# Plain float32 for the first group's second product, and silu written over h in PSUM

## The chip, the cores and the metric

The kernel runs on one core of one Trainium2 chip. The metric is the device time of one execution in microseconds (us). Before the change three runs took 1640.9, 1642.14 and 1642.24 us, a median of 1642.14.

## What is computed

Pooled attention (keys and values averaged over 8 neighbours, 8 batches, 8 heads, 576 positions of 64), then two MLPs on the 4608 rows of 512, with a hidden width of 2048. The first MLP has the silu, the second h * clip(h + 3, 0, 6) / 6:

```
def _moe_ref(x, w_in, w_out):
    h = x @ w_in
    g = h * (1.0 / (1.0 + np.exp(-h)))
    return (g @ w_out).astype(np.float32)

def _moe2_ref(x, w_in, w_out):
    h = x @ w_in
    g = h * np.clip(h + 3.0, 0.0, 6.0) / 6.0
    return (g @ w_out).astype(np.float32)

x = attention(q, k, v) as 4608 x 512
return _moe2_ref(_moe_ref(x, w_in1, w_out1), w_in2, w_out2)
```

The weights arrive as float64, so as pairs of 32-bit words, and are made into float32 on the chip.

## The kernel before

The 4608 rows are 36 tiles of 128, in 9 groups of 4 tiles (512 rows). The hidden width is 16 blocks f of 128. The program has three stages: the attention of the first four tiles (to about 33 us), the first MLP group by group with the attention of the next group's tiles woven in (to about 920 us), and the second MLP by a Strassen-like scheme (to the end). The change touches the first MLP.

An iteration (g, f) of the first MLP issues, in this order and by hand, since the schedule is the order of the code:

- TensorE (PE): `h_mm`, 12 matmuls of 512 columns into one of two PSUM banks (`hps`, L479). Operands are float32r; each is split into a high and a low part (`xh`, `xl`, and `whl` for weights), and three of the four partial products are taken.
- ScalarE (ACT) and VectorE (DVE): `act_a` takes tanh(h/2) (L491) and (tanh + 1) * h (L492) into an SBUF tile `t`; `act_b` splits it into `gh` (ACT, L500) and `gl` = t - gh (DVE, L501).
- PE: `y_mm` of the iteration before (`pend`), 12 matmuls (L522), three partial products for each of four banks `y0` to `y3`. After the last f, `y_out` empties those banks (L532 on ACT, L534 on DVE), and the next group's first `y_mm` writes them again.

In the first group (g = 0) the first MLP's 32 weight tiles are also made, in the order of `pieces`: in-tile f, out-tile f - 1, and so on. A tile's 512 KB of words land in `wraw` (two words an element). `split_a` makes float32 of them: L108 on ACT, L111 and L114 on DVE, then either L121 on DVE or, with `mul`, L110 on ACT and L119 on GpSimd (POOL). The result, `wmag`, one of 4 buffers, goes to `split_b`: L131 on ACT copies the high part into `whl`, L132 on POOL subtracts the low part. `whl` takes the place of `wraw`. `share` says how many tiles an iteration converts: 1 to 3.

From the second group on the same iterations convert the second MLP's weights in small pieces (L156 to L178), at their own pace.

The attention of tile t in group 0 goes in threes of iterations: scores (L340) in the first, transposes of the probabilities (L404) in the second, the weighted sum (L444) and the split of x (L460, L461) in the third. The normalising (L388 to L393 on DVE) ends the first.

The tile `t` has two buffers, taken in turn. A buffer is free for the next writer when its last reader is done.

```
def act_a(layer, ps):                                        # before
    t = p2.tile([P, GT], F32, tag="t", name="t")             # two buffers
    nc.scalar.activation(t2, h, AF.Tanh, scale=0.5)          # ACT, reads PSUM
    nc.vector.scalar_tensor_tensor(out=t2, in0=t2, scalar=1.0, in1=h, ...)
def act_b(layer, g, f, t):
    nc.scalar.activation(gh, t, AF.Copy)
    nc.vector.tensor_tensor(out=gl, in0=t, in1=gh.bitcast(F32), op=ALU.subtract)
```

Of the kernel before, what the change touches and what calls it, by code (L numbers as in the profile page):

```python
# [25 lines left out]
def kernel(  # L26
# [57 lines left out]
    def dealt(ps):  # L84
        return ps.rearrange("p (n a) -> p a n", a=2)

    def in_two(ap):
        return ap.rearrange("p (a n) -> p a n", a=2)
# [12 lines left out]
    def split_a(layer, f, piece, mul=False):  # L101


        raw = w_raw.pop((layer, f, piece))
        hw = raw[:, :, 1]
        mag = att.tile([P, DM], F32, tag="wmag", name="wmag", bufs=4)
        bits = mag.bitcast(U32)
        nc.scalar.activation(mag, hw.bitcast(F32), AF.Copy, scale=2.0 ** -112)  # L108
        if mul:
            nc.scalar.activation(hw.bitcast(F32), hw.bitcast(F32), AF.Sign)  # L110
        nc.vector.tensor_scalar(  # L111
            out=bits, in0=bits, scalar1=3, scalar2=None, op0=ALU.logical_shift_left
        )
        nc.vector.scalar_tensor_tensor(  # L114
            out=bits, in0=raw[:, :, 0], scalar=29, in1=bits,
            op0=ALU.logical_shift_right, op1=ALU.bitwise_or,
        )
        if mul:
            nc.gpsimd.tensor_tensor(out=mag, in0=mag, in1=hw.bitcast(F32), op=ALU.mult)  # L119
        else:  # L120
            nc.vector.scalar_tensor_tensor(  # L121
                out=bits, in0=hw, scalar=0x80000000, in1=bits,
                op0=ALU.bitwise_and, op1=ALU.bitwise_or,
            )
        w_mag[layer, f, piece] = mag

    def split_b(layer, f, piece):

        mag = w_mag.pop((layer, f, piece))
        t = wts.tile([P, 2, DM], F32R, tag=f"{'io'[piece]}{f}", name="whl")  # L130
        nc.scalar.activation(t[:, 0, :], mag, AF.Copy)  # L131
        nc.gpsimd.tensor_tensor(out=t[:, 1, :], in0=mag, in1=t[:, 0, :].bitcast(F32), op=ALU.subtract)  # L132
        if piece == 0:
            t = t.rearrange("p a (c f) -> p a c f", f=P)
        w_sl[layer, f, piece] = (t[:, 0], t[:, 1])
# [337 lines left out]
    def h_mm(layer, g, f):  # L473
        ih, il = w_sl[layer, f, 0]
        xh, xl = xs[layer * NG + g]
        ps = ps_h.tile([P, GT], F32, tag="h", name="hps")
        for n, (w, x) in enumerate(((ih, xh), (il, xh), (ih, xl))):
            for c in range(NKC):
                nc.tensor.matmul(  # L479
                    ps,  # L480
                    w[:, c, :],
                    shuffled(x[:, c, :]),
                    start=(c == 0 and n == 0),
                    stop=(c == NKC - 1 and n == 2),
                )
        return ps

    def act_a(layer, ps):
        t = p2.tile([P, GT], F32, tag="t", name="t")
        t2, h = in_two(t), dealt(ps)  # L490
        nc.scalar.activation(t2, h, AF.Tanh, scale=0.5)  # L491
        nc.vector.scalar_tensor_tensor(  # L492
            out=t2, in0=t2, scalar=1.0, in1=h, op0=ALU.add, op1=ALU.mult
        )
        return t

    def act_b(layer, g, f, t):
        gh = p2.tile([P, GT], F32R, tag="gh", name="gh")
        gl = p2.tile([P, GT], F32R, tag="gl", name="gl")
        nc.scalar.activation(gh, t, AF.Copy)  # L500
        nc.vector.tensor_tensor(out=gl, in0=t, in1=gh.bitcast(F32), op=ALU.subtract)  # L501
        g_t[layer, g, f] = (gh, gl)


    FIRST = (0, 1)
    LAST = (NF - 1, NF - 2)

    def y_mm(layer, g, f):
        gh, gl = g_t.pop((layer, g, f))
        oh, ol = w_sl[layer, f, 1]  # L510
        if f == FIRST[layer]:
            y_ps[layer, g] = [
                ps_y.tile([P, 512], F32, tag=f"y{i}", name=f"y{i}") for i in range(4)
            ]
        for i, ps in enumerate(y_ps[layer, g]):
            sl = slice(i * P, (i + 1) * P)
            if layer == 0:
                prods = ((oh[:, sl], gh), (ol[:, sl], gh), (oh[:, sl], gl))
            else:
                prods = ((gh[:, sl], oh), (gh[:, sl], ol), (gl[:, sl], oh))  # L520
            for n, (a, b) in enumerate(prods):
                nc.tensor.matmul(  # L522
                    ps, a, shuffled(b), start=(f == FIRST[layer] and n == 0),
                    stop=(f == LAST[layer] and n == 2),
                )
# [126 lines left out]
    with tc.manual_schedule():  # L652
# [105 lines left out]
        for layer in range(1):  # L758
            for g in range(NG):
                todo = stages(g)  # L760
                if g == NG - 1:
                    early.close()
                    open_late()
                for f in range(NF):
                    n = (layer * NG + g) * NF + f
                    now = dict(todo[f])
                    load_ahead(2)
                    if n >= NF:
                        while ahead2 and len(half_raw) < 3:
                            load_half(*ahead2.pop(0))  # L770
                    while later:
                        later.pop(0)()
                    ps = h_mm(layer, g, f)
                    if 1 in now:
                        t1 = now[1]
                        scores(t1)
                        if t1 + 1 < NTILE:
                            load_q(t1 + 1)
                    if 3 in now:
                        pv = weighted(now[3])  # L780
                    tt = act_a(layer, ps)
                    quota = share[n] if n < NF else 2
                    due = len(done)
                    conv_a(1, 0)
                    for job in jobs_b:
                        job()
                    jobs_b = []
                    act_b(layer, g, f, tt)
                    if NF <= n < (NG - 1) * NF and SPLITTING[f] and jobs:
                        key, jobs_b = jobs.pop(0)  # L790
                        if key:
                            half_a(*key)
                    if g == NG - 1:
                        if f == 0:
                            load_x1(0)
                        elif f % 2 == 0 and f < 12:
                            make_x(0, f // 2 - 1)
                    conv_b(due)
                    if 1 in now:
                        new_pr(t1)  # L800
                        below_max(t1, 0)
                        below_max(t1, 1)
                        exps(t1, 0)
                        exps(t1, 1)
                    if 3 in now:
                        split_x(now[3], pv)
                    if n < 3:
                        for j in ((0, 1), (2,), (3,))[n]:
                            pool_k(1, j)
                    if 1 <= n < 5:  # L810
                        pool_v(1, n - 1)
                    if pend is not None:
                        y_mm(*pend)
                        if pend[2] == NF - 1:
                            y_out(*pend[:2])
                    pend = (layer, g, f)
                    conv_a(quota - 1, 1)
                    if 1 in now:
                        norm(t1)
                    if 4 in now:  # L820
                        vector_T(now[4])
                    if 2 in now:
                        probs_T(now[2])
                    if n >= 5 and f % 2 == 1:
                        for b, j in kv_wait:
                            pool_k(b, j)
                            pool_v(b, j)
                        kv_wait = []
                        if kv_jobs and f % 4 == 1 and TPG * (g + 1) + f // 4 + 4 >= first_tile[kv_jobs[0][0]]:
                            b, j = kv_jobs.pop(0)  # L830
                            load_k(b, j)
                            load_v(b, j)
                            kv_wait.append((b, j))
                    s = n - (NG - 1) * NF - 1
                    if 0 <= s < NF:
                        if s < 4:
                            load_factor(0, PASSING[s])
                        else:
                            load_factor((s - 4) // 3, STAYING[(s - 4) % 3])
                        load_split(s)  # L840
# [134 lines left out]
```

## Time and profile before

| | before |
|---|---|
| median of three runs | 1642.14 us |
| the profiled execution | 1641.74 us |
| its span, first to last instruction | 1639.9 us |
| PE busy | 1585.7 us (97%) |
| DVE, ACT, POOL busy | 1029.6, 632.9, 383.5 us |
| mean granted clock of PE | 0.989 of full speed |

A busy PE is not a PE at its peak, and the share over the whole span hides that the stages differ: in the first 180 us PE has gaps and a granted clock under 1, after that hardly any. Rows name a line, an engine, an operation and out<-in; the bracket after a row is the idle time in front of it and what ended it.

### The profile page before, as it was taken

The numbers are of one execution on the slowest core, as the hardware profiler recorded it, in microseconds if no ns is written. First come the engines' busy times: TensorE is split into PE (matmuls) and PEld (weight loads), VectorE is DVE, ScalarE is ACT, GpSimd is POOL, SyncE is SP. The second block draws the span as 40 slices with busy tenths as digits, with TensorE's granted clock in tenths as the row PEclk, the third lists the DMA queues.
The fourth block names the chain that finished last, engine by engine and source line by source line (L and its number), as shares of the span: only waits on it lengthen the run. The fifth ranks groups of instructions, "written<-read, shape, count | busy, mean of one in ns | idle before, by whom it ended". The sixth has DMA issues, their size and how long they took to land.

```text
span 1639.9 us, 24118 instructions
## 1 busy us (share of the span) xinstructions
PE 1585.7 (97%) x9312; PEld 1409.8 (86%) x9312; DVE 1029.6 (63%) x1608; ACT 632.9 (39%) x1094; POOL 383.5 (23%) x377
## 2 busy tenths in 40 slices
PE   7786999999999999999999999999999999999999
PEld 6565888888888888888888899999999999999998
DVE  6999677676766677675632455555555555656464
ACT  5345433333333333333322333333443343433333
POOL 4755222221322132311111011212121203020200
PEclk9899999999999999999999999999999999999999
DMA  9251334443444444433255634343435343535341
GB/s 316 78 197 37 109 99 162 133 153 124 147 143 138 136 135 140 157 126 123 70 179 201 228 114 155 104 159 111 154 107 160 107 154 103 157 100 167 102 130 52
DMA packets 101330, 224.27 MB, mean 137 GB/s; under 512 B 10464, under 2 KB 35936, under 8 KB 101216
## 3 DMA queue, kind: packets, MB, share of 16 engines
q1 hardware_dynamic: 101216, 222.73, 41.7%
q8 instruction: 73, 1.20, 0.3%
q14 instruction: 41, 0.34, 0.1%
HBM read 169.74 MB, written 52.95 MB: 136 GB/s over the span
## 4 chain that ended last, share of the span: by engine, by line
PE 77%; DVE 13%; DMA 3%; ACT 3%; issue 2%; SPq 0%; ACTq 0%; DVEq 0%
PE y L522 40%; PE hps L479 19%; PE p L597 16%; PE aps L340 1%; PE aps L444 1%; DVE u L864 1%; ACT gh L620 1%; DVE wmag L111 1%; DVE gl L621 1%; DVE gl L501 1%; DVE wmag L114 1%; DVE t L613 1%; DVE kbd L271 1%; DVE wmag L121 1%; ACT t L612 1%
## 5 line engine op out<-in xcount | busy, mean ns | idle before, releaser
L479 PE MATMUL hps<-x,whl 128*128 128x512 f32 x1728 | 398.7, 380 | 4.2 <-POOL whl L132 2.1
L597 PEld LDWEIGHTS p<-xst,wst 128*128 128x128 f32 x3024 | 359.6, 192 | 14.9 <-DVE u L864 7.8
L479 PEld LDWEIGHTS hps<-x,whl 128*128 128x128 f32 x1728 | 327.2, 190 | 51.7 <-POOL whl L132 2.5
L597 PE MATMUL p<-xst,wst 128*128 128x256 f32 x3024 | 363.2, 275 | 4.5 <-DVE u L864 4.5
L522 PE MATMUL y<-gh,whl 128*128 128x512 f32 x1152 | 358.6, 393 | 1.5 <-POOL whl L132 1.1
L522 PE MATMUL y<-whl,gh 128*128 128x512 f32 x1152 | 343.1, 379 | 0.6 <-ACT gh L620 0.6
L522 PEld LDWEIGHTS y<-gh,whl 128*128 128x128 f32 x1152 | 218.0, 194 | 37.9 <-issue 5.4
L522 PE MATMUL y<-gl,whl 128*128 128x512 f32 x576 | 224.3, 389 | 14.0 <-DVE gl L501 13.9
L585 POOL TENSOR_TENSOR xst<-xr,xst 128x512 fp32r<-128x512 f32 x63 | 83.4, 1324 | 619.1 <-ACT xst L584 619.1
L522 PEld LDWEIGHTS y<-whl,gh 128*128 128x128 f32 x1152 | 207.3, 190 | 24.2 <-ACT gh L620 0.8
L522 PE MATMUL y<-whl,gl 128*128 128x512 f32 x576 | 218.4, 379 | 0.1
L621 DVE TENSOR_TENSOR gl<-t,gh 128x512 fp32r<-128x512 f32 x144 | 115.1, 799 | 131.4 <-ACT gh L620 131.4
L492 DVE SCALAR_TENSOR_TENSOR t<-t,hps 128x512 f32<-128x512 f32 x144 | 97.7, 678 | 153.7 <-ACT t L491 152.9
L491 ACT ACTIVATE t<-hps 128x512 f32<-128x512 f32 x144 | 85.7, 595 | 275.3 <-PE hps L479 275.0
L501 DVE TENSOR_TENSOR gl<-t,gh 128x512 fp32r<-128x512 f32 x144 | 128.4, 892 | 90.5 <-ACT gh L500 90.5
L174 POOL TENSOR_TENSOR hs<-hmag,hs 128x256 fp32r<-128x256 f32 x88 | 65.1, 744 | 470.8 <-ACT hs L173 398.5
L620 ACT ACTIVATE gh<-t 128x512 fp32r<-128x512 f32 x144 | 120.3, 835 | 127.1 <-DVE t L613 127.1
L500 ACT ACTIVATE gh<-t 128x512 fp32r<-128x512 f32 x144 | 90.7, 630 | 181.8 <-DVE t L492 181.1
L613 DVE SCALAR_TENSOR_TENSOR t<-t,u 128x512 f32<-128x512 f32 x108 | 90.9, 842 | 104.8 <-ACT t L612 104.8
L864 DVE TENSOR_TENSOR u<-u,p 128x512 f32<-128x512 f32 x180 | 120.0, 683 | 44.7 <-PE p L597 40.5
L612 ACT ACTIVATE t<-u,three 128x512 f32<-128x512 f32 x108 | 77.8, 720 | 172.2 <-DVE u L864 172.2
L522 PEld LDWEIGHTS y<-gl,whl 128*128 128x128 f32 x576 | 111.9, 194 | 34.3 <-DVE gl L501 17.8
(86 smaller groups left out, 1358.6 us busy)
## 6 DMA issues: line engine op xcount, KB each, us to landing
wst<-ws SPq DMA_DIRECT2D x156, 512.0 KB
ws<-hs SPq DMA_DIRECT2D x56, 256.0 KB
bl<-bT SPq DMA_DIRECT2D x28, 384.0 KB
x<-o SPq DMA_DIRECT2D x36, 256.0 KB
xr<-x SPq DMA_DIRECT2D x36, 256.0 KB
out_dram<-o SPq DMA_DIRECT2D x36, 256.0 KB
wraw<-in_moe_w_in_dram SPq DMA_DIRECT2D x16, 512.0 KB
wraw<-in_moe_w_out_dram SPq DMA_DIRECT2D x16, 512.0 KB
```

What stands on the lines that cost most here:

```text
L479: nc.tensor.matmul(ps, w[:, c, :], shuffled(x[:, c, :]), start=(c == 0 and n == 0), stop=(c == NKC - 1 and n == 2),)
L491: nc.scalar.activation(t2, h, AF.Tanh, scale=0.5)
L492: nc.vector.scalar_tensor_tensor(out=t2, in0=t2, scalar=1.0, in1=h, op0=ALU.add, op1=ALU.mult)
L500: nc.scalar.activation(gh, t, AF.Copy)
L501: nc.vector.tensor_tensor(out=gl, in0=t, in1=gh.bitcast(F32), op=ALU.subtract)
L522: nc.tensor.matmul(ps, a, shuffled(b), start=(f == FIRST[layer] and n == 0), stop=(f == LAST[layer] and n == 2),)
L597: nc.tensor.matmul(ps[:, j * HW:(j + 1) * HW], w[:, j, a, c, :], shuffled(x[:, b, c, :]), start=(j == 0 and n == 0 and c == 0), stop=(j == ...
L612: nc.scalar.activation(t, h, AF.Relu, bias=three)
L613: nc.vector.scalar_tensor_tensor(out=t, in0=t, scalar=6.0, in1=h, op0=ALU.min, op1=ALU.mult)
L620: nc.scalar.activation(oh, t3, AF.Copy)
L621: nc.vector.tensor_tensor(out=ol, in0=t3, in1=oh.bitcast(F32), op=ALU.subtract)
L864: nc.vector.tensor_tensor(out=out, in0=a, in1=b, op=ALU.add)
```

## The change

In the first group `y_mm` becomes `y_whole`: four matmuls instead of twelve, with both operands in plain float32, not split. `act_b` is not run there. The out-tiles of the first MLP are converted by `split_a` as before, but the last step writes the float32 values over the high words in `wraw` (every second word), and `y_whole` reads them there. `split_b` of these 16 tiles moves to the second group: `split_whole(f)`, at the start of iteration (1, f), copies the tile into a buffer of `t` (L140) and then splits it (L150 on ACT, L151 on POOL). From the second group on `act_a` writes (tanh + 1) * h over h in PSUM (L518), and `act_b` reads PSUM (L526, L527).

```diff
+        dst = raw[:, :, 1] if piece else None
...
         if mul:
-            nc.gpsimd.tensor_tensor(out=mag, in0=mag, in1=hw.bitcast(F32), op=ALU.mult)
+            nc.gpsimd.tensor_tensor(
+                out=mag if dst is None else dst.bitcast(F32), in0=mag, in1=hw.bitcast(F32),
+                op=ALU.mult,
+            )
         else:
             nc.vector.scalar_tensor_tensor(
-                out=bits, in0=hw, scalar=0x80000000, in1=bits,
+                out=bits if dst is None else dst, in0=hw, scalar=0x80000000, in1=bits,
...
+        if piece:
+            w_whole[f] = dst.bitcast(F32)
+        else:
+            w_mag[layer, f, piece] = mag
+    def split_whole(f):
+        mag = p2.tile([P, DM], F32, tag="t", name="wcopy")
+        nc.scalar.activation(mag, w_whole.pop(f), AF.Copy)
+        w_mag[0, f, 1] = mag
+        split_b(0, f, 1)
...
+        if (layer, f, piece) not in w_mag:
+            return
...
+        if g == 0:
+            nc.scalar.activation(in_two(t), dealt(ps), AF.Tanh, scale=0.5)
+            nc.vector.scalar_tensor_tensor(
+                out=in_two(t), in0=in_two(t), scalar=1.0, in1=dealt(ps), op0=ALU.add, op1=ALU.mult
+            )
+            return t
+        nc.scalar.activation(t, ps, AF.Tanh, scale=0.5)
         nc.vector.scalar_tensor_tensor(
+            out=ps, in0=t, scalar=1.0, in1=ps, op0=ALU.add, op1=ALU.mult
+        )
+        return ps
...
+        nc.scalar.activation(in_two(gh), dealt(ps), AF.Copy)
+        nc.vector.tensor_tensor(
+            out=in_two(gl), in0=dealt(ps), in1=in_two(gh).bitcast(F32), op=ALU.subtract
+        )
+    def y_whole(f):
+        t, w = g_t.pop((0, 0, f)), w_whole[f]
+        if f == 0:
+            y_ps[0, 0] = [ps_y.tile([P, 512], F32, tag=f"y{i}", name=f"y{i}") for i in range(4)]
+        for i, ps in enumerate(y_ps[0, 0]):
+            nc.tensor.matmul(
+                ps, w[:, i * P:(i + 1) * P], shuffled(t), start=(f == 0), stop=(f == NF - 1)
+            )
...
+                    if g == 1:
+                        split_whole(f)
                     ps = h_mm(layer, g, f)
...
-                    act_b(layer, g, f, tt)
+                    if g:
+                        act_b(layer, g, f, tt)
+                    else:
+                        g_t[0, 0, f] = tt
```

DVE in the first group, from the silu of f = 4 to that of f = 5. Before, where L492 is the silu, L111 to L121 convert weights and L501 is `gl`:

```order
L492 SCALAR_TENSOR_TENSOR t<-t,hps 128x512
L111 TENSOR_SCALAR wmag<-wmag 128x512
L114 SCALAR_TENSOR_TENSOR wmag<-wraw,wmag 128x512
L121 SCALAR_TENSOR_TENSOR wmag<-wraw,wmag 128x512
L501 TENSOR_TENSOR gl<-t,gh 128x512
L111 TENSOR_SCALAR wmag<-wmag 128x512
L114 SCALAR_TENSOR_TENSOR wmag<-wraw,wmag 128x512
L111 TENSOR_SCALAR wmag<-wmag 128x512
L114 SCALAR_TENSOR_TENSOR wmag<-wraw,wmag 128x512
L121 SCALAR_TENSOR_TENSOR wmag<-wraw,wmag 128x512
L492 SCALAR_TENSOR_TENSOR t<-t,hps 128x512
```

After, the same stretch, with the silu at L513 and the conversion at L113 to L126:

```order
L513 SCALAR_TENSOR_TENSOR t<-t,hps 128x512
L113 TENSOR_SCALAR wmag<-wmag 128x512
L116 SCALAR_TENSOR_TENSOR wmag<-wraw,wmag 128x512
L126 SCALAR_TENSOR_TENSOR wraw<-wraw,wmag 128x512
L113 TENSOR_SCALAR wmag<-wmag 128x512
L116 SCALAR_TENSOR_TENSOR wmag<-wraw,wmag 128x512
L113 TENSOR_SCALAR wmag<-wmag 128x512
L116 SCALAR_TENSOR_TENSOR wmag<-wraw,wmag 128x512
L126 SCALAR_TENSOR_TENSOR wraw<-wraw,wmag 128x512
L513 SCALAR_TENSOR_TENSOR t<-t,hps 128x512
```

`gl` is gone; the last step of the out-tiles writes `wraw`.

POOL at the end of the first group and the start of the second. Before (L132 is the low part of a weight tile, L119 the sign by multiplication, L281 to L283 the pooling of v, L174 the second MLP's weights):

```order
L132 TENSOR_TENSOR whl<-wmag,whl 128x512 x3
L119 TENSOR_TENSOR wmag<-wmag,wraw 128x512
L132 TENSOR_TENSOR whl<-wmag,whl 128x512 x2
L281 TENSOR_TENSOR vraw<-vraw 72x2x256
L282 TENSOR_TENSOR vraw<-vraw 72x2x128
L283 TENSOR_TENSOR vp_82<-vraw 72x128
L174 TENSOR_TENSOR hs<-hmag,hs 128x256
```

After (L151 is the low part now, L193 the second MLP's weights):

```order
L151 TENSOR_TENSOR whl<-wmag,whl 128x512 x2
L121 TENSOR_TENSOR wraw<-wmag,wraw 128x512
L300 TENSOR_TENSOR vraw<-vraw 72x2x256
L301 TENSOR_TENSOR vraw<-vraw 72x2x128
L302 TENSOR_TENSOR vp_82<-vraw 72x128
L151 TENSOR_TENSOR whl<-wcopy,whl 128x512 x4
L193 TENSOR_TENSOR hs<-hmag,hs 128x256
```

The subtractions of the out-tiles (`whl<-wcopy`) stand behind the first group, one an iteration.

ACT across the same border. Before (L491 tanh, L500 `gh`, L364 the exponentials of the next tile, L532 emptying `y0` and `y2`):

```order
L491 ACTIVATE t<-hps 128x512
L500 ACTIVATE gh<-t 128x512
L491 ACTIVATE t<-hps 128x512
L500 ACTIVATE gh<-t 128x512
L364 ACTIVATE pr_84<-pr_84 128x288 x2
L532 ACTIVATE o<-y_614 128x512
L532 ACTIVATE o<-y_616 128x512
L491 ACTIVATE t<-hps 128x512
```

After (L512 and L517 tanh, L526 `gh`, L140 and L150 the copies of `split_whole`):

```order
L512 ACTIVATE t<-hps 128x512
L140 ACTIVATE wcopy<-wraw 128x512
L150 ACTIVATE whl<-wcopy 128x512
L517 ACTIVATE t<-hps 128x512
L526 ACTIVATE gh<-hps 128x512
L383 ACTIVATE pr_84<-pr_84 128x288 x2
L572 ACTIVATE o<-y_597 128x512
L572 ACTIVATE o<-y_599 128x512
L140 ACTIVATE wcopy<-wraw 128x512
```

In the first iteration of the second group the tanh (L517) writes the buffer that the last `y_whole` of the first group reads, and the emptying of the y banks stands behind it.

## Rows read from the trace of the kernel before

**Rows 1.** Windows of three rounds: length, busy (count) PE, PEld, DVE, ACT, POOL, clock, DMA.
```profile
83.35:111.37 28.02, 22.70 (x120) 18.23 (x120) 27.00 (x32) 14.48 (x25) 16.44 (x11) 0.88 0.72 269
...
139.67:168.00 28.33, 21.09 (x104) 17.41 (x104) 27.26 (x34) 14.42 (x25) 14.81 (x11) 0.91 0.11 31
sum 84.65, PE 65.41 PEld 53.63 DVE 81.49 ACT 43.07 POOL 47.49; mean PE 21.80 PEld 17.88 DVE 27.16 ACT 14.36 POOL 15.83
```

**Rows 2.** Groups on PE, 83.35 to 168.0 us: busy, mean ns, idle before, releaser.
```profile
L522 PE MATMUL y<-gl,whl 128*128 128x512 f32 x36 | 16.8, 467 | 6.6 <-DVE gl L501 6.6
```

**Rows 3.** Groups on DVE, 83.35 to 168.0 us.
```profile
L114 DVE SCALAR_TENSOR_TENSOR wmag<-wraw,wmag 128x512 uint32<-128x512 uint32 x18 | 19.5, 1085 | 0.6
L121 DVE SCALAR_TENSOR_TENSOR wmag<-wraw,wmag 128x512 uint32<-128x512 uint32 x12 | 14.8, 1235 | 0.4
L501 DVE TENSOR_TENSOR gl<-t,gh 128x512 fp32r<-128x512 f32 x9 | 14.7, 1628 | 0.0
L111 DVE TENSOR_SCALAR wmag<-wmag 128x512 uint32<-128x512 uint32 x18 | 13.9, 773 | 0.0
L492 DVE SCALAR_TENSOR_TENSOR t<-t,hps 128x512 f32<-128x512 f32 x9 | 6.1, 682 | 0.1
```

**Rows 4.** Groups on POOL, 83.35 to 168.0 us.
```profile
L132 POOL TENSOR_TENSOR whl<-wmag,whl 128x512 fp32r<-128x512 f32 x18 | 30.3, 1704 | 28.2 <-ACT whl L131 28.2
L119 POOL TENSOR_TENSOR wmag<-wmag,wraw 128x512 f32<-128x512 f32 x6 | 7.8, 1294 | 6.2 <-ACT t L491 3.7 <-DVE wmag L114 2.6
```

**Rows 5.** Timeline of POOL and of DVE, 32 and 114 us: start, length.
```profile
32.10 1.27 POOL L132 TENSOR_TENSOR whl<-wmag,whl 128x512 fp32r<-128x512 f32 x1 [12.79 <-ACT whl L131]
...
113.31 1.93 POOL L132 TENSOR_TENSOR whl<-wmag,whl 128x512 fp32r<-128x512 f32 x1 [6.63 <-ACT whl L131]
114.05 1.74 DVE L501 TENSOR_TENSOR gl<-t,gh 128x512 fp32r<-128x512 f32 x1
115.72 0.42 DVE L111 TENSOR_SCALAR wmag<-wmag 128x512 uint32<-128x512 uint32 x1
116.17 0.69 DVE L114 SCALAR_TENSOR_TENSOR wmag<-wraw,wmag 128x512 uint32<-128x512 uint32 x1
```

**Rows 6.** Group `gl` on DVE, 33 to 83.35 us.
```profile
L501 DVE TENSOR_TENSOR gl<-t,gh 128x512 fp32r<-128x512 f32 x4 | 7.0, 1745 | 0.0
```

**Rows 7.** Timeline of PE: plain float32 (ident, kbd), then float32r (hps).
```profile
11.11 2.85 PE L328 MATMUL aps<-ident 128*128 128x128 f32 x24
13.79 4.09 PE L340 MATMUL aps<-kbd,stage 128*128 128x144 f32 x32
187.61 2.75 PE L479 MATMUL hps<-x,whl 128*128 128x512 f32 x12
```

**Rows 8.** Timeline of PE: the attention's part of a round.
```profile
83.58 1.04 PE L404 MATMUL aps<-ident,pr 128*72 128x128 f32 x8 [1.88 <-DVE pr L393]
88.07 1.05 PE L444 MATMUL aps<-pT,vp 72*64 72x64 f32 x28 [0.86 <-ACT pT L405]
97.97 1.44 PE L340 MATMUL aps<-kbd,qT 128*128 128x144 f32 x8
```

**Rows 9.** Timeline where the second group starts.
```profile
184.30 0.60 ACT L491 ACTIVATE t<-hps 128x512 f32<-128x512 f32 x1 [3.26 <-PE hps L479]
184.93 0.69 PE L522 MATMUL y<-gh,whl 128*128 128x512 f32 x2
186.32 0.69 DVE L501 TENSOR_TENSOR gl<-t,gh 128x512 fp32r<-128x512 f32 x1 [0.70 <-ACT gh L500]
189.11 1.06 ACT L532 ACTIVATE o<-y 128x512 f32<-128x512 f32 x2
190.20 0.59 PE L522 MATMUL y<-gh,whl 128*128 128x512 f32 x2
```

**Rows 10.** Window of the second group.
```profile
182.00:280.00 98.00, 97.07 (x506) 83.46 (x505) 68.23 (x124) 34.99 (x70) 23.55 (x29) 1.00 0.41 133
```

**Rows 11.** Group on PE, 182 to 911 us: matmuls on `gl`.
```profile
L522 PE MATMUL y<-gl,whl 128*128 128x512 f32 x508 | 193.1, 380 | 0.1
```

More of the change, by code (lines that the diff above doesn't have):

```diff
@@ L118, in split_a @@
         if mul:
-            nc.gpsimd.tensor_tensor(out=mag, in0=mag, in1=hw.bitcast(F32), op=ALU.mult)
+            nc.gpsimd.tensor_tensor(
+                out=mag if dst is None else dst.bitcast(F32), in0=mag, in1=hw.bitcast(F32),
+                op=ALU.mult,
+            )
         else:
             nc.vector.scalar_tensor_tensor(
-                out=bits, in0=hw, scalar=0x80000000, in1=bits,
+                out=bits if dst is None else dst, in0=hw, scalar=0x80000000, in1=bits,
                 op0=ALU.bitwise_and, op1=ALU.bitwise_or,
             )
-        w_mag[layer, f, piece] = mag
+        if piece:
+            w_whole[f] = dst.bitcast(F32)
+        else:
+            w_mag[layer, f, piece] = mag
+    w_whole = {}
+    def split_whole(f):
[3 more added lines that the diff above has]
+        split_b(0, f, 1)
     def split_b(layer, f, piece):
+        if (layer, f, piece) not in w_mag:
+            return
         mag = w_mag.pop((layer, f, piece))
@@ L486, in h_mm, with act_a, act_b @@
         return ps
-    def act_a(layer, ps):
+    def act_a(g, ps):
         t = p2.tile([P, GT], F32, tag="t", name="t")
-        t2, h = in_two(t), dealt(ps)
-        nc.scalar.activation(t2, h, AF.Tanh, scale=0.5)
+        if g == 0:
[5 more added lines that the diff above has]
+        nc.scalar.activation(t, ps, AF.Tanh, scale=0.5)
         nc.vector.scalar_tensor_tensor(
-            out=t2, in0=t2, scalar=1.0, in1=h, op0=ALU.add, op1=ALU.mult
+            out=ps, in0=t, scalar=1.0, in1=ps, op0=ALU.add, op1=ALU.mult
         )
-        return t
-    def act_b(layer, g, f, t):
+        return ps
+    def act_b(layer, g, f, ps):
         gh = p2.tile([P, GT], F32R, tag="gh", name="gh")
         gl = p2.tile([P, GT], F32R, tag="gl", name="gl")
-        nc.scalar.activation(gh, t, AF.Copy)
-        nc.vector.tensor_tensor(out=gl, in0=t, in1=gh.bitcast(F32), op=ALU.subtract)
+        nc.scalar.activation(in_two(gh), dealt(ps), AF.Copy)
+        nc.vector.tensor_tensor(
+            out=in_two(gl), in0=dealt(ps), in1=in_two(gh).bitcast(F32), op=ALU.subtract
+        )
         g_t[layer, g, f] = (gh, gl)
@@ L506 @@
     LAST = (NF - 1, NF - 2)
+    def y_whole(f):
[6 more added lines that the diff above has]
+            )
     def y_mm(layer, g, f):
+        if (layer, g) == (0, 0):
+            return y_whole(f)
         gh, gl = g_t.pop((layer, g, f))
@@ L780 @@
                         pv = weighted(now[3])
-                    tt = act_a(layer, ps)
+                    tt = act_a(g, ps)
                     quota = share[n] if n < NF else 2
```

## The prediction

> **What bounds the kernel now.** I read the windows first, since the page's shares mix stages. In the first MLP's first group one round of three iterations repeats: from one silu behind the normalising to the next such silu takes 28.0 to 28.3 us, and of the 84.65 us of three rounds DVE is busy 81.5 us, while PE's granted clock is 0.88 to 0.91 [rows 1]. So DVE sets the pace there. [...] Then the later groups: PE is busy 97.07 of 98 us in the second group, at a clock of 1.00, and from 182 to 911 us it waits 0.1 us in all for `gl` [rows 10, 11]. There PE sets the pace and the others have room.
>
> Why DVE is slow is read from durations. A `gl` takes 0.69 us where POOL is idle [rows 9] but 1.63 us in the rounds [rows 3]. The timeline shows how: one that started at 114.05 ended at 115.79, 0.55 us behind the end of POOL's subtraction at 115.24, and right after it the same engine's L111 and L114 take 0.42 and 0.69 us [rows 5], where their means are 0.77 and 1.09 [rows 3]. DVE waits out POOL's instruction. The silu, which has one operand in PSUM, stays at 0.68 [rows 3].
>
> [...]
>
> **The rounds.** Free durations: 0.69 for `gl`, L114 and (same form) L121, 0.42 for L111. Waiting for POOL in three rounds: `gl` 9 x (1.628 - 0.69) = 8.5, L114 18 x (1.085 - 0.69) = 7.1, L121 12 x (1.235 - 0.69) = 6.5, L111 18 x (0.773 - 0.42) = 6.4 us, together 28.5 [rows 3]. POOL's work there, with L132 at its free 1.27 us [rows 5]: 18 x 1.27 = 22.9, L119 7.8, and 47.5 - 30.3 - 7.8 = 9.4 for the pooling of v: 40.1 us [rows 1, 4]. That is 0.71 us of DVE waiting for each us of POOL work. The change takes out nine `gl` (6.2 us of own time) and nine of the 18 subtractions (11.4 us of POOL, so 8.1 us of waiting). DVE's 84.65 us become 70.4.
>
> Can PE follow? Plain float32: 24 rows of 128 columns in 2.85 us, 32 of 144 in 4.09 [rows 7]. In the program these are 12 and 16 matmuls, so each counts as two rows. With the last row's tail off (about 0.28), 4.09 gives 123 ns a row, 0.85 ns a column, 436 ns for 512 columns; the other row gives 112 ns, 447. A `y_whole` is eight rows, 3.5 us (3.6 by the other). Float32r is 12 in 2.75 [rows 7], 2.6 us from start to start, for `h_mm` and for the old `y_mm` alike. So a y costs PE 0.9 us more. A round on PE: 3 x 2.6 + 3 x 3.5 + attention (about 0.8, 1.05 and 1.2, and a wait of 0.86 for ACT) [rows 8] = 22.2 us, three 66.6. DVE at 70.4 stays the slower, but by 5%, so that each hitch of one meets the other; I add 1 us: 71.4, a gain of 13.3. Bounds: 6.2 if the other DVE instructions now wait for all that POOL still does (only `gl`'s own time goes), 18 if PE is the floor.
>
> **Before and after the rounds.** From the first silu to 83.35 us stand four iterations with four `gl` of 1.745 us [rows 6]; their own time is 2.8 us, and five out-tiles' subtractions leave POOL, 5 x 1.27 x 0.71 = 4.5. I take 6.8 (bounds 2.8 and 9.5). Behind the rounds the conversion is over and PE sets the pace: y(13), y(14) and y(15) cost 0.9 us more each, a loss of 2.7. ACT loses `gh` and a copy per iteration in this group; it was busy 43.1 of 84.65 us [rows 1], so that counts nothing. Writing every second word costs DVE and POOL nothing by my reading, since their input there already has that step; if it did, it would be part of the waiting, whose bounds stand.
>
> **The border to the second group.** Here the change adds a wait. The tanh of (1, 0) writes the `t` buffer of (0, 15), which the last `y_whole` reads; that y follows `h_mm` (1, 0) on PE. Before, tanh started at 184.30, y(0, 15) at 184.93 [rows 9]; now tanh starts when that y ends, 184.93 + 3.5 + 0.15 = 188.6 on the old time scale, 4.3 us later. Queued behind it are, on DVE, silu, `gl`, the maxima of the next tile, two emptyings of y banks; on ACT, `gh`, two exponentials, two emptyings. The first of ACT's ended at 189.11 + 0.53 = 189.64 [rows 9] and now ends at 193.95. `y_mm` (1, 0) writes that bank; PE wants it at 190.20 + 0.9 = 191.1. A stall of 2.9 us (bounds 0 and 3.8).
>
> **The second group.** 16 subtractions of 1.27 us and 32 copies of about 0.6 come in. ACT goes from 35 to 55 of 98 us, POOL from 24 to 44. At the rate above DVE waits 20.3 x 0.71 = 14.4 us more, 68.2 becomes 82.6 of 98 [rows 10], less what `gl` waited. The moved step issues no DMA; on POOL it goes ahead of the second MLP's subtractions (L193), whose stores then leave 1.3 us later, with nobody waiting for them in this stage. An iteration's weights are wanted only behind the next `h_mm`. I price a few late `gl` at 0.6 us (bounds 0 and 8). Silu in PSUM: no instruction more, and the bank is held until `gl` is done, but the next `h_mm` into it follows the y that needs that `gl` anyway: 0 (bounds -0.5 and 1). The second MLP is untouched: 0.
>
> **The sum**, against the profiled execution's 1641.7 us (span 1639.9 and 1.8 around it; 0.4 under the median): -13.3 - 6.8 + 2.7 + 2.9 + 0.6 = -13.9, so 1627.8, and 1628 on the median's scale.
>
> **Rivals.** First, the waiting nearly vanishes and PE is the floor: -18 - 9.5 + 2.7 + 2.9 + 0.6 gives 1620.8. For it: POOL would have long gaps; against: L132 and L119 still fall among the conversions. Second, waiting is only passed on: -6.2 - 2.8 + 6.2 gives 1639. For it: in rows 3 every two-operand instruction waits, whichever is nearest; against: POOL's work itself shrinks by a fourth. Third, the second group isn't covered: half a us lost in each of 16 iterations instead of 0.6 in all gives 1635; for it, DVE at 84%, and that ACT's copy needs a `t` buffer which POOL must have read; against, the 0.1 us of rows 11. Fourth, on the slower side: `y_whole` is dearer and PE becomes the bound of the first group. With y the cost of one, three rounds take 9y + 35 us, the sum is 9y + 35 - 84.65 - 6.8 + 3(y - 2.6) + 3.5 = 12y - 61 us; it turns positive at y = 5.1 us, 635 ns a row instead of 436, and passes the limit of what can be told at 5.4. [...] For it: the clock of 0.88 and the 467 ns; and no row shows weights read at every second word in plain float32. Against: the lower level came behind gaps, and the wait for `gl` that made the largest of them goes.
>
> [...]
>
> **Chances.** Forecast 0.47 (1622 to 1634), first rival 0.18, second 0.15, third 0.12, fourth 0.08. The range leaves out the fourth's upper part and the tails: 1616 to 1640. What can be told from no change is about 0.2%, 3.3 us, so faster means under 1638.9: forecast, first and third, half of the second, a little of the fourth: 0.86. Same 0.09, slower 0.05.
>
> **What would show it.** Rounds of about 23.8 us instead of 28.2, with nine conversions' worth of `gl` rows gone; POOL's L151 at half the count there, and the means of L116 and L126 below 1.0 us; PE's clock above 0.9; `y_whole` rows about 436 ns apart; at the border a PE wait near 2.9 us for ACT's L572; `gl` (L527) at about 0.69 in all later groups, with no change of their length. The forecast is wrong if y rows are much over 500 ns apart, if the rounds stay over 26 us, or if PE waits in more than one or two iterations of the second group.

## The result: 17.6 us faster, by other terms than predicted

| | before | after |
|---|---|---|
| median, us | 1642.19 (1640.9 to 1642.97, 4 runs) | 1624.59 (1623.38 to 1625.27, 4 runs) |
| ratio, 95% interval | | 0.9893 [0.9876, 0.991] |
| profiled execution: time / span, us | 1641.7 / 1639.9 | 1624.84 / 1623.1 |
| three rounds of the first group, us | 84.65 | 71.33 |

The time is 3.4 us under the forecast of 1628 and within its range. Cut into the terms of the prediction, by the starts of the same instructions in both traces (the silu of f = 4 and of f = 13, `h_mm` of (1, 1), the second MLP's first product), the two spans differ like this:

| stretch | predicted, us | measured, us |
|---|---|---|
| to the silu of f = 4 (83.35, now 76.32) | -6.8 | -7.0 |
| three rounds, to the silu of f = 13 | -13.3 | -13.3 |
| from there to `h_mm` (1, 1) (19.61, now 26.79) | +2.7 | +7.2 |
| stall behind it, at the border | +2.9 | 0 |
| `h_mm` (1, 1) to the second MLP (726.4, now 722.6) | +0.6 | -3.8 |
| the rest | 0 | +0.2 |
| sum | -13.9 | -16.7 |

(The spans themselves differ by 16.8; the rows are rounded.) 0.5 us of the last `y_whole` shows only behind the start of `h_mm` (1, 1), so the later groups alone are 4.3 us shorter. The cut by DVE's silu also moves work between the rows: on PE, `h_mm` (0, 5) starts 3.9 us earlier than before (80.43 against 84.37), from there to `h_mm` (0, 14) 13.9 us are gained, and from there to `h_mm` (1, 1) 4.7 us are lost.

The rounds took the predicted time, but not from the predicted engine. Three windows of the changed kernel, against [rows 1], with the same columns (length, busy and count of PE, PEld, DVE, ACT, POOL, clock, DMA):

```profile
76.32:100.02 23.70, 23.70 (x109) 14.21 (x108) 20.34 (x29) 10.40 (x20) 10.36 (x8) 1.00 0.80 297
100.02:123.83 23.81, 23.81 (x93) 14.05 (x92) 20.83 (x30) 10.55 (x20) 10.63 (x8) 1.00 0.19 62
123.83:147.65 23.82, 23.82 (x93) 14.05 (x92) 20.82 (x31) 10.54 (x20) 9.79 (x8) 1.00 0.12 37
sum 71.33, PE 71.33 PEld 42.31 DVE 62.00 ACT 31.49 POOL 30.77; mean PE 23.78 PEld 14.10 DVE 20.67 ACT 10.50 POOL 10.26
```

PE is busy 71.33 of 71.33 us at a granted clock of 1.00. DVE, which set the pace before with 81.5 of 84.65 us, now has 9.3 us to spare. A PE that is always busy may be slow or wanted, so the length of its rows comes next. All rows of `y_whole` by their line (duration least / median / most, first and last start), and then one y in the timeline of PE with two of its weight loads (start, length):

```profile
L542 PE MATMUL y<-t,wraw x128: 700/703/1222, 44.1 to 174.4; 128*128 128x512 f32 x128
```

```profile
84.28 4.59 PE L542 MATMUL y<-t,wraw 128*128 128x512 f32 x8
...
84.93 0.20 PEld L542 LDWEIGHTS y<-t,wraw 128*128 128x128 f32 x1 [0.34 <-issue]
85.47 0.20 PEld L542 LDWEIGHTS y<-t,wraw 128*128 128x128 f32 x1 [0.34 <-issue]
```

The loads start 0.54 us apart, each behind a matmul, so a row costs 541 ns and a y eight of them, 4.33 us: 0.83 us more than the 3.5 us predicted. (The 703 ns of one row reach 162 ns into the next row.) The weight load of 0.2 us lies within the 541 ns.

DVE's groups in the three rounds, against [rows 3], with busy time, mean ns, and idle time before them:

```profile
L116 DVE SCALAR_TENSOR_TENSOR wmag<-wraw,wmag 128x512 uint32<-128x512 uint32 x18 | 18.3, 1015 | 0.6
L113 DVE TENSOR_SCALAR wmag<-wmag 128x512 uint32<-128x512 uint32 x18 | 8.9, 493 | 0.0
L126 DVE SCALAR_TENSOR_TENSOR wraw<-wraw,wmag 128x512 uint32<-128x512 uint32 x6 | 8.1, 1344 | 0.2
L126 DVE SCALAR_TENSOR_TENSOR wmag<-wraw,wmag 128x512 uint32<-128x512 uint32 x6 | 7.0, 1166 | 0.2
L513 DVE SCALAR_TENSOR_TENSOR t<-t,hps 128x512 f32<-128x512 f32 x10 | 6.9, 686 | 6.2 <-ACT t L512 6.2
```

The last row is the one to read for the bound: DVE now waits 6.2 us for ACT's tanh, and the tanh waits for PE's `hps` (L512, 24.6 us). `gl` is gone, and POOL's subtraction stands at 9 instead of the 18 of [rows 4]:

```profile
L151 POOL TENSOR_TENSOR whl<-wmag,whl 128x512 fp32r<-128x512 f32 x9 | 14.0, 1559 | 23.5 <-ACT whl L150 23.5
```

At the border, with the columns of [rows 9]:

```profile
168.89 1.27 POOL L151 TENSOR_TENSOR whl<-wcopy,whl 128x512 fp32r<-128x512 f32 x1 [12.76 <-ACT whl L150]
170.20 0.60 ACT L517 ACTIVATE t<-hps 128x512 f32<-128x512 f32 x1 [1.38 <-POOL whl L151]
170.64 4.48 PE L542 MATMUL y<-t,wraw 128*128 128x512 f32 x8
...
174.44 3.27 PE L498 MATMUL hps<-x,whl 128*128 128x512 f32 x12
177.54 0.59 PE L562 MATMUL y<-gh,whl 128*128 128x512 f32 x2
```

The tanh of (1, 0) starts before the last y of the first group, not behind it. It waited 1.38 us for POOL's subtraction, that is, for the buffer of `wcopy`, not for the `t` of (0, 15). So the two buffers are not "taken in turn", as the description of the kernel has it and as the prediction and the text on ACT's order took it. The first y of the second group follows `h_mm` (1, 1) without a gap.

From the second group on, `gl` has its free duration in every one of its 128 rows (least 690, most 694 ns); the kernel before had 819 ns in the mean there. The groups on DVE, before (182 to 911 us) and after (whole program):

```profile
L501 DVE TENSOR_TENSOR gl<-t,gh 128x512 fp32r<-128x512 f32 x127 | 104.0, 819 | 88.4 <-ACT gh L500 88.4
```

```profile
L527 DVE TENSOR_TENSOR gl<-hps,gh 128x512 fp32r<-128x512 f32 x128 | 88.5, 691 | 85.1 <-ACT gh L526 85.1
```

### The profile page after: what moved, and what is told of

Its sections match the earlier page's. It is cut to its first block, busy times and chain, and to the rows that moved or that the text cites. A ratio compares the mean times of both kernels' runs of the same rounds, so it can differ in the third digit from the quotient of the medians.

```text
span 1623.1 us, 24092 instructions
## 1 busy us (share of the span) xinstructions
PE 1596.5 (98%) x9248; PEld 1390.3 (86%) x9248; DVE 987.2 (61%) x1592; ACT 632.4 (39%) x1094; POOL 367.3 (23%) x377
## 4 chain that ended last, share of the span: by engine, by line
PE 87%; DVE 6%; DMA 3%; ACT 2%; issue 1%; SPq 0%; ACTq 0%; DVEq 0%
PE y L562 41%; PE hps L498 22%; PE p L637 16%; PE y L542 4%; PE aps L359 2%; PE aps L463 2%; DVE u L909 1%; ACT gh L660 1%; DVE gl L661 1%; DVE t L653 1%; ACT t L652 1%; DVE o L574 1%; DMA wraw<-in_moe_w_out_dram 1%; DMA stage<-in_v_dram 1%; DMA qT<-in_q_dram 1%
## 5 line engine op out<-in xcount | busy, mean ns | idle before, releaser
L562 PE MATMUL y<-gh,whl 128*128 128x512 f32 x1024 | 310.0, 384 | 0.0
L562 PEld LDWEIGHTS y<-gh,whl 128*128 128x128 f32 x1024 | 189.4, 189 | 29.4 <-issue 3.1
L661 DVE TENSOR_TENSOR gl<-t,gh 128x512 fp32r<-128x512 f32 x144 | 115.4, 802 | 131.5 <-ACT gh L660 131.5
L562 PE MATMUL y<-gl,whl 128*128 128x512 f32 x512 | 194.6, 380 | 0.0
L518 DVE SCALAR_TENSOR_TENSOR hps<-t,hps 128x512 f32<-128x512 f32 x128 | 88.2, 689 | 169.0 <-ACT t L517 168.5
L517 ACT ACTIVATE t<-hps 128x512 f32<-128x512 f32 x128 | 76.3, 596 | 263.7 <-PE hps L498 262.1
L660 ACT ACTIVATE gh<-t 128x512 fp32r<-128x512 f32 x144 | 120.4, 836 | 127.1 <-DVE t L653 127.1
L193 POOL TENSOR_TENSOR hs<-hmag,hs 128x256 fp32r<-128x256 f32 x88 | 64.2, 734 | 410.4 <-ACT hs L192 380.8
L527 DVE TENSOR_TENSOR gl<-hps,gh 128x512 fp32r<-128x512 f32 x128 | 88.5, 691 | 85.1 <-ACT gh L526 85.1
L526 ACT ACTIVATE gh<-hps 128x512 fp32r<-128x512 f32 x128 | 76.6, 598 | 125.3 <-DVE hps L518 125.3
L562 PEld LDWEIGHTS y<-whl,gl 128*128 128x128 f32 x576 | 108.9, 189 | 15.9 <-DVE gl L661 0.5
```

Of the source, the lines that this page charges most:

```text
L518: nc.vector.scalar_tensor_tensor(out=ps, in0=t, scalar=1.0, in1=ps, op0=ALU.add, op1=ALU.mult)
L526: nc.scalar.activation(in_two(gh), dealt(ps), AF.Copy)
L527: nc.vector.tensor_tensor(out=in_two(gl), in0=dealt(ps), in1=in_two(gh).bitcast(F32), op=ALU.subtract)
L562: nc.tensor.matmul(ps, a, shuffled(b), start=(f == FIRST[layer] and n == 0), stop=(f == LAST[layer] and n == 2),)
L660: nc.scalar.activation(oh, t3, AF.Copy)
L661: nc.vector.tensor_tensor(out=ol, in0=t3, in1=oh.bitcast(F32), op=ALU.subtract)
```

## Experiments

Two questions were open: why a row of `y_whole` costs 541 ns, and which part made the later groups shorter. The theories' names in the quoted expectations: M and W hold the access pattern of the moving or of the stationary operand (the weights) responsible for the 541 ns, P plain float32 itself; K says that silu in PSUM made the later groups shorter, T that shifted times of transfers did; B says that the border stall comes once the buffers are in turn, N that it doesn't.

**1. The moving operand read in a row.** In the first group tanh and silu write `t` in h's own order, so `y_whole` reads it without taking its columns in turn from the two halves.

```diff
-            nc.scalar.activation(in_two(t), dealt(ps), AF.Tanh, scale=0.5)
+            nc.scalar.activation(t, ps, AF.Tanh, scale=0.5)
-                out=in_two(t), in0=in_two(t), scalar=1.0, in1=dealt(ps), op0=ALU.add, op1=ALU.mult
+                out=t, in0=t, scalar=1.0, in1=ps, op0=ALU.add, op1=ALU.mult
-                ps, w[:, i * P:(i + 1) * P], shuffled(t), start=(f == 0), stop=(f == NF - 1)
+                ps, w[:, i * P:(i + 1) * P], t, start=(f == 0), stop=(f == NF - 1)
```

> The changed kernel, but t of the first group is kept in h's own column order and y_whole reads it straight through, instead of in turn from two halves; the weights stay at every second word. The changed kernel's rounds are 23.8 us with PE busy throughout, and a plain float32 row of y_whole takes 541 ns instead of my 436. Theory M (the alternating moving read costs the 105 ns): rows fall to about 436 ns, a round to about 21.5 us (PE 21.3, DVE's own 21.5), total about 1624.6 - 7 to - 11 = 1614 to 1618 us. Theory W (the weights at every second word cost it) and theory P (plain float32 at 512 columns simply costs it): rows stay at 541 ns, rounds at 23.8, total 1624 to 1626 us.

Measured: 1614.88 us (1614.33 to 1615.41), ratio to the kernel before 0.9829 [0.9812, 0.9845]. The rows of y by their line, and the weight loads on PE's second queue in one y:

```profile
L542 PE MATMUL y<-t,wraw x128: 592/592/1223, 46.3 to 166.1; 128*128 128x512 f32 x128
```

```profile
84.98 0.20 PEld L542 LDWEIGHTS y<-t,wraw 128*128 128x128 f32 x1 [0.23 <-issue]
85.41 0.20 PEld L542 LDWEIGHTS y<-t,wraw 128*128 128x128 f32 x1 [0.23 <-issue]
```

703 ns become 592, and the rows start 0.43 us apart instead of 0.54. The prediction's 436 ns was worked out from rows whose moving operand is read in a row; for such an operand it is right. It is also the lowest median of all that ran, 9.7 us below the changed kernel's. Its windows:

```profile
79.80:101.01 21.21, 21.21 (x110) 14.22 (x109) 20.18 (x29) 10.30 (x20) 10.55 (x8) 1.00 0.77 281
101.01:123.30 22.29, 21.43 (x94) 14.12 (x93) 21.22 (x31) 10.34 (x20) 9.76 (x9) 1.00 0.24 84
123.30:145.40 22.10, 21.32 (x94) 13.98 (x92) 21.03 (x31) 10.03 (x20) 9.45 (x9) 1.00 0.13 39
```

A round takes 21.2 to 22.3 us, and in each neither PE nor DVE is idle for more than 1.1 us.

**2. The weights without gaps.** The last step of the conversion writes the float32 weights side by side instead of over every second word.

```diff
-        dst = raw[:, :, 1] if piece else None
+        dst = raw.rearrange("p f w -> p (f w)")[:, :DM] if piece else None
```

> The changed kernel, but the float32 values of w_out are written side by side into the first half of the raw tile, so that y_whole's weights are read without a step; the moving read stays as changed. Theory W: rows of y_whole fall from 541 to about 436 ns, rounds to about 21.5 us, total 1614 to 1618 us. Theories M and P: rows stay at 541 ns, total 1624 to 1626 us.

Measured: 1627.14 us (1625.63 to 1628.79), 0.9905 [0.989, 0.992]. Rows of y:

```profile
L542 PE MATMUL y<-t,wraw x128: 700/703/1223, 45.0 to 175.7; 128*128 128x512 f32 x128
```

Still 703 ns: weights at every second word cost this matmul nothing, and W falls. The time is 1.1 us above the expected range and 2.5 us above the changed kernel's median, though the intervals of the two ratios overlap. By the starts of `h_mm` in the two traces 1.3 us of it are there by the end of the first group (0.9 already before the first y, 45.0 against 44.1 us), where it is not shown why; 1.8 us come in the one iteration (1, 4) of the second group, told under 5 and 6; and 0.5 us are won back later.

**3. Both.** The edits of 1 and 2 together.

> Both edits at once: moving read straight through and weights side by side. Theory P: rows stay at 541 ns and the total at 1624 to 1626 us. Theory M or W: as the one of the two runs that helps, 1614 to 1618 us; if each costs a part, this one is the only one that comes to 436 ns.

Measured: 1616.94 us (1615.38 to 1618.86), 0.9843 [0.9828, 0.9858]; 592 ns, as in 1. Nothing is left for the weights.

**4. How fast is DVE, if PE has room?** From f = 1 on `y_whole` multiplies 256 of its 512 columns; half of the first group's y is left out.

```diff
+            n = GT if f == 0 else GT // 2
-                ps, w[:, i * P:(i + 1) * P], shuffled(t), start=(f == 0), stop=(f == NF - 1)
+                ps[:, :n], w[:, i * P:(i + 1) * P], shuffled(t)[:, :n // 2], start=(f == 0), stop=(f == NF - 1)
```

> The changed kernel, but from f = 1 on y_whole multiplies 256 of its 512 columns (the rest of the first group's y is left out). This frees PE, so that what DVE alone would set in the rounds is seen. If DVE's floor is its busy time plus its waits for ACT's exponentials (62.0 + 1.5 + 0.9 us of gaps in three rounds of the changed kernel), a round takes 21.5 us, against 23.8 with the full y_whole and 23.5 by my prediction's estimate of DVE (70.4 us in three). If PE was not the bound, the rounds stay at 23.8 us. Total about 1614 to 1618 us, the tail after the rounds being shorter too by about 1 us an iteration.

Measured, one run: 1616.44 us. The window of three rounds (columns as above), and DVE's groups there:

```profile
76.68:142.97 66.29, 56.41 (x292) 44.63 (x292) 63.13 (x90) 32.93 (x58) 30.87 (x25) 0.94 0.39 140
```

```profile
L116 DVE SCALAR_TENSOR_TENSOR wmag<-wraw,wmag 128x512 uint32<-128x512 uint32 x18 | 19.5, 1083 | 0.6
L113 DVE TENSOR_SCALAR wmag<-wmag 128x512 uint32<-128x512 uint32 x18 | 12.4, 690 | 0.0
...
L126 DVE SCALAR_TENSOR_TENSOR wraw<-wraw,wmag 128x512 uint32<-128x512 uint32 x6 | 6.3, 1052 | 0.2
L126 DVE SCALAR_TENSOR_TENSOR wmag<-wraw,wmag 128x512 uint32<-128x512 uint32 x6 | 5.7, 950 | 0.2
```

DVE, busy 63.13 of 66.29 us, is the bound again: 22.1 us a round, where the prediction had 23.5 and the expectation 21.5. (In experiment 1, with the whole y, three rounds took 65.6 us, so this is no fixed floor.) Its waiting for POOL, against the free durations that the prediction used: L116 18 x (1.083 - 0.69) = 7.1, L113 18 x (0.690 - 0.42) = 4.9, L126 6 x 0.362 + 6 x 0.26 = 3.7, in all 15.7 us. POOL's work there is 30.87 less the 10 x 0.25 by which L151 was itself stretched, 28.4 us. That is 0.55 us of waiting per us, not 0.71. `gl` alone had 8.5 of the 28.5 us of waiting before; the change took out the instruction that waited longest each time, 0.94 us. Without `gl` the others waited 20.0 us for 40.1 us of POOL before, a rate of 0.50: it was the average with `gl` in it that could not be carried over.

**5 and 6. The two parts apart.** One kernel has only the first part (the first group's y in float32, `split_b` moved; silu to SBUF in all groups); the other has only the second part, put into the kernel before. The core of the first one's edit:

```diff
-        nc.scalar.activation(t, ps, AF.Tanh, scale=0.5)
+        nc.scalar.activation(in_two(t), dealt(ps), AF.Tanh, scale=0.5)
-            out=ps, in0=t, scalar=1.0, in1=ps, op0=ALU.add, op1=ALU.mult
+            out=in_two(t), in0=in_two(t), scalar=1.0, in1=dealt(ps), op0=ALU.add, op1=ALU.mult
-        return ps
+        return t
```

And of the second one's:

```diff
+        if g == 0:
...
-            out=t2, in0=t2, scalar=1.0, in1=h, op0=ALU.add, op1=ALU.mult
+            out=ps, in0=t, scalar=1.0, in1=ps, op0=ALU.add, op1=ALU.mult
-        return t
+        return ps
```

> Only the first part of the change: the first group as changed, but from the second group on the silu goes to t in SBUF and is split from there, as before. Between the first y of the second group and the second MLP the changed kernel is 4.3 us shorter than before, where I had put 0. Theory K (gl with an operand in PSUM no longer waits for POOL, so DVE comes earlier to the pooled keys and PE's waits for them, 2.1 us on PE and 3.4 us on its weight loads before, go): this kernel loses most of it, and also meets the 16 added POOL subtractions with a gl that waits: total 1624.6 + 3 to + 6 = 1628 to 1631 us. Theory T (the 4.3 us come from the shifted times of transfers, not from PSUM): 1624 to 1626 us.

> Only the second part: the kernel before, with the silu written over h in PSUM from the second group on; the first group and the weights as before. Theory K: gl falls from 0.82 to 0.69 us in the later groups, PE's waits for pooled keys fall from 2.1 us to under 0.5, and the total is 1642.2 - 2 to - 4.5 = 1638 to 1640 us. Theory T, and my prediction's term of 0 (-0.5 to +1): 1641.7 to 1643 us.

Measured, beside 1642.13 for the kernel before:

| | median, us | ratio | `h_mm` (1, 1) to the second MLP, us |
|---|---|---|---|
| first part only | 1633.75 (1632.23 to 1633.86) | 0.9941 [0.9929, 0.9954] | 175.62 to 905.97 = 730.4 |
| second part only | 1638.13 (1637.02 to 1640.09) | 0.9971 [0.996, 0.9982] | 188.93 to 911.21 = 722.3 |
| both | 1624.59 | 0.9893 [0.9876, 0.991] | 174.44 to 897.01 = 722.6 |
| neither | 1642.19 | | 187.61 to 913.97 = 726.4 |

What PE's matmuls waited for in this stretch (engine, tile and line, releaser; us in all, times, longest), the kernel before, first part only, second part only, and both:

```profile
PE aps L340 <- DVE kbd L271: 2.1, 4, 0.9
PE aps L340 <- DVE x L461: 0.3, 1, 0.3
```

```profile
PE aps L359 <- DVE kbd L290: 2.2, 4, 0.9
PE aps L359 <- DVE x L480: 2.1, 3, 1.1
```

```profile
PE aps L340 <- DVE kbd L271: 0.4, 1, 0.4
```

```profile
PE aps L359 <- DVE kbd L290: 0.2, 1, 0.2
PE aps L359 <- DVE x L480: 0.2, 1, 0.2
```

And the weight loads' longest wait for DVE, before:

```profile
PEld aps L340 <- DVE kbd L271: 3.4, 5, 1.1
```

PE hardly waits for `gl` itself (0.1 us in [rows 11]), but in a few iterations it waits for the pooled keys (`kbd`) or the next x, which stand behind `gl` on the same queue of DVE. With `gl` at 0.691 us instead of a mean of 0.82 those waits nearly vanish. Compared iteration by iteration, the second part alone wins 4.1 us in this stretch, 3.4 of them at the scores (L340), which wait for `kbd` and x. So silu in PSUM is worth 4 us by itself, inside K's range, where the prediction had 0 and a bound of -0.5.

With the first part it is worth 9.2 (1633.75 - 1624.59), more than K's 3 to 6. In the traces 1.2 us of that stand ahead of `h_mm` (1, 1), where the two programs are the same, and 7.8 behind it. From the third group on it is 2.8 us, by the same waits (3.0 in the kernel with the second part only). The other 5.0 us fall in the second group, 4.2 of them in the one iteration (1, 4). There a DVE step of the second MLP's weights (L179) lasts 2.54 us beside a moved subtraction, x and `kbd` behind it come late, PE waits 1.07 and 0.90 us, and pairs of matmuls of the y behind these gaps last 1.16 to 1.01 us instead of 0.59, which costs 1.7 us more:

```profile
193.55 2.54 DVE L179 SCALAR_TENSOR_TENSOR hmag<-hraw,hmag 128x256 uint32<-128x256 uint32 x1
...
193.86 1.27 POOL L151 TENSOR_TENSOR whl<-wcopy,whl 128x512 fp32r<-128x512 f32 x1
```

It would be wrong to put this down to `gl` reading SBUF. In the same iteration of experiments 2, 3 and 4, where `gl` reads PSUM, the next step (L183) lasts 2.47 to 2.48 us, and the iteration is 1.8, 1.8 and 3.9 us longer than in the changed kernel. Experiment 2, and then the changed kernel:

```profile
193.49 2.47 DVE L183 SCALAR_TENSOR_TENSOR hmag<-hraw,hmag 128x256 uint32<-128x256 uint32 x1
193.73 1.26 POOL L151 TENSOR_TENSOR whl<-wcopy,whl 128x512 fp32r<-128x512 f32 x1
```

```profile
192.20 0.60 DVE L183 SCALAR_TENSOR_TENSOR hmag<-hraw,hmag 128x256 uint32<-128x256 uint32 x1
192.47 1.47 POOL L151 TENSOR_TENSOR whl<-wcopy,whl 128x512 fp32r<-128x512 f32 x1
```

DVE's step starts 0.24 us ahead of the subtraction in the one and 0.27 us in the other; so small a difference goes with 1.8 us of PE's time. The moved subtractions are free in the changed kernel, then, but not by their place in the schedule. The parts alone give -8.4 and -4.0, together -17.6; that the two together give more is mostly this one iteration.

**7. The border stall brought about.** The two `t` buffers strictly in turn, so that the tanh of (1, 0) must take the one that the last `y_whole` reads.

```diff
+    def t_in_turn(name):
+        turn_of[0] += 1
+        return p2.tile([P, GT], F32, tag=f"t{turn_of[0] % 2}", name=name, bufs=1)
-        mag = p2.tile([P, DM], F32, tag="t", name="wcopy")
+        mag = t_in_turn("wcopy")
-        t = p2.tile([P, GT], F32, tag="t", name="t")
+        t = t_in_turn("t")
```

> The changed kernel with the two buffers of t made strictly alternating in program order, as my prediction took them to be. In the changed kernel the tanh of iteration (1, 0) starts at 170.20, before the last y_whole (170.64), because it takes the buffer of the copied weights, which POOL has read by then. Theory B (the stall of 2.9 us that I priced was right in its mechanism, and only the buffer was another): here tanh waits until that y ends at about 175, PE waits about 3 us at the first y of the second group, total 1627 to 1628 us. Theory N (no such stall even then, since the emptying of the y banks is covered): 1624 to 1625 us.

Measured: 1629.85 us (1628.36 to 1630.22), 0.9919 [0.9906, 0.9933]. The timeline at the border:

```profile
170.71 4.48 PE L547 MATMUL y<-t,wraw 128*128 128x512 f32 x8
...
175.23 0.60 ACT L522 ACTIVATE t<-hps 128x512 f32<-128x512 f32 x1 [6.34 <-PE y L547]
...
180.00 1.07 ACT L577 ACTIVATE o<-y 128x512 f32<-128x512 f32 x2
180.63 1.22 PE L567 MATMUL y<-gh,whl 128*128 128x512 f32 x2 [2.85 <-ACT o L577]
182.07 1.06 PE L567 MATMUL y<-gh,whl 128*128 128x512 f32 x2
```

Here is the predicted stall, 2.85 us for a forecast of 2.9, link by link: y ends, tanh starts, the emptying of the bank comes late, PE waits. Behind the gap pairs of matmuls last 1.06 to 1.22 us instead of 0.59, which adds to it; the window behind the gap, with the columns of [rows 1], has a mean granted clock of 0.63:

```profile
180.63:184.90 4.27, 4.27 (x13) 3.48 (x14) 3.66 (x9) 2.49 (x5) 1.48 (x1) 0.63 0.70 256
```

The iteration is 4.7 us longer than in the changed kernel, of which later iterations win back 1.0: the second MLP starts at 900.66 instead of 897.01, 3.65 us later. The median is above B's 1627 to 1628, and the medians differ by 5.3 us, of which this trace explains no more than 3.65.

## Why the prediction was right, and where it was wrong

**The direction and the total** came out, the total partly by luck: the size of a y, the rate of DVE's waiting, the tail, the border stall and the worth of silu in PSUM were all off, and their errors partly cancelled. The y rows are 541 ns apart, on the side of 500 that the prediction itself had named as a sign of being wrong.

**"A `y_whole` is eight rows, 3.5 us"** was the mis-sized step. It is eight rows of 541 ns, 4.33 us. The trace of before had no row of plain float32 with a moving operand read in turn from two halves; I took the pattern to be free from float32r, which read so takes 216 ns a row. The moving-operand experiment shows its price, 111 ns of 703; the weights at every second word have none (703 ns with and without gaps). The float32r row could not be carried to another type; why plain float32 pays for the pattern, and why float32r read from two halves takes no more than 216 ns, is not shown. Thus the mechanism of the fourth rival, PE as the bound of the first group, came true, short of its turning point of 5.1 us.

**The rounds' 71.4 us** were met at 71.33 by luck, with two errors against each other: DVE would need about 66 (66.3 in experiment 4, with 0.55 us of waiting per us of POOL, not 0.71), which is less than the 70.4 predicted, and PE needs 71.3 instead of 66.6. Nine y cost it 7.5 us more, and the wait for ACT of 0.86 us a round, which the estimate kept, is gone. The 1 us added for hitches between the two wasn't wanted.

**The tail, "a loss of 2.7"**, counted three y at 0.9 us each. The three cost 4.33 - 2.6 = 1.73 us each, 5.2, of which 0.5 show behind `h_mm` (1, 1). Another 3.1 us are y(12): before, DVE came so late that only 0.35 us of it were left behind the silu of f = 13, now 3.5. The transposes, eight in 1.68 us at a granted clock of 0.52 before (L404, at 168.35 us) and in 1.04 us at 1.00 now (L423, at 151.14 us), give back 0.6. That makes the 7.2.

**The stretch before the rounds** gave 7.0 for 6.8 by DVE's silu. PE still has 3.3 us of y(3) to do at that point, where before it had none, and this comes back as y(12) in the tail. No run takes the stretch's two terms apart.

**The border stall of 2.9** didn't come. The chain was right, as experiment 7 shows; the assumption that the tanh takes the buffer of (0, 15) was not. It got the one that `wcopy` had used. The order of instructions doesn't show which buffer a tile gets, and I had not worked that out.

**Silu in PSUM, "0 (bounds -0.5 and 1)"** was -4.0 us alone. The step that failed is to give a faster `gl` no worth because PE does not wait for it: [rows 11] shows 0.1 us of waiting for `gl`, but the waits that count were those for `kbd` (2.1 us on PE before, 0.4 with the second part only), on DVE's queue behind `gl`. I looked for the waits on the instruction that becomes faster and not for those on its successors. The forecast of 0.69 us for `gl` there came true. The trace of before has no `gl` with an operand in PSUM, only the silu with one at 0.68 us [rows 3]; in the changed kernel all 128 rows take 0.69 us, and 50 of them lie beside an instruction of POOL. Of the 127 before, from 182 to 911 us, 45 lie beside one, with 1.05 us in the mean and 1.71 at most; the others take 0.69.

**The second group, 0.6**, is covered in the changed kernel, but by a hair. In experiments 2 to 4 one iteration of it costs 1.8 to 3.9 us more, and 4.2 with the first part only. That is a piece of the third rival, in one iteration instead of 16 and by waits for x and `kbd` instead of its named `t` buffer.

**Of what should show it**, means of L116 and L126 below 1.0 us didn't come: they are 1.02, and 1.34 and 1.17 in L126's two groups. With PE faster, in experiment 4, L126 has 1.05 and 0.95, while L113 rises from 0.49 to 0.69. Which instruction meets POOL depends on the pace, so the mean of one line was a poor sign; the sum of the waiting is a better one. The later groups did change their length, by those 4.3 us.

## What to carry to other kernels

When an operand changes its type, price its access pattern anew from a row of the same type and pattern, or bound the price by the nearest one; here a row of 541 ns became one of 429, and a change in layout of three lines was worth another 10 us. An engine for whose instruction nobody waits may still delay the next ones on its queue, as `gl` (0.1 us of PE's waiting) did with `kbd` (2.1 us): look for waits on everything behind it before costing it at nothing. DVE's waiting for POOL was not proportional to POOL's work, 0.71 us of it per us with `gl` and 0.55 without in experiment 4: a rate averaged over several instructions did not hold once the one that waits longest was taken out. And when two totals or two terms agree, compare the stretches by the engine that now sets the pace too: the 7.0 for 6.8 and the 71.33 for 71.4 hid an error each.

## What the hardware showed that I had not expected

A moving operand taken in turn from two halves of a tile, 1 KB apart, cost plain float32 a quarter more here (541 against 430 ns for 512 columns, from experiment 1's durations of 703 and 592 and the starts of the loads). Float32r read in the same way took 216 ns a row (12 matmuls in 2.6 us from start to start, for `h_mm` and the old y); no run here reads float32r straight through at this width. But the trace of before has a row that I had overlooked. The program starts with dummy matmuls on a float32r tile of zeros (`probe`), the last ten of them taken in turn from four quarters, 512 bytes apart. They last 448 ns instead of 379, and start 283 instead of 216 ns apart, at a granted clock of 1.00 (8.3 to 10.8 us), so float32r was slower in that pattern, too:

```profile
L321 PE MATMUL aps<-probe x10: 444/448/448, 8.3 to 10.8; 128*128 128x512 f32 x10
```

```profile
L479 PE MATMUL hps<-x,whl x1728: 379/379/792, 33.0 to 911.2; 128*128 128x512 f32 x192
```

Weights read at every second word cost nothing that shows: loads of 195 ns against 190, beside rows of 541, and equal matmuls (703 ns). In experiment 7 a gap of 2.85 us on PE was followed by a lower granted clock (0.63 in the mean over the next 4.27 us), though PE had been busy at 1.00 from 170.7 to 177.5 us ahead of it. In the trace of before, too, the lower level of which the fourth rival speaks came behind gaps: the clock was 0.52 from 91.0 to 94.5 us, behind a wait of 1.62 us, and 0.50 from 108.29 to 111.0 us, behind one of 2.26 us for `gl`; the matmuls of y started 0.43 us apart there instead of 0.216.
